# Closing an expert's first tile earlier, and GpSimd's weight sums in four pieces

## The chip, the cores and the metric

The kernel runs on one core of a Trainium2 chip. The metric is the device time of one execution in microseconds (us); the time of a kernel is the median of its runs.

## The reference

Sliding window attention (8 batches, 8 heads, 576 tokens, head size 64, window 64), whose output becomes 4608 rows of 512, followed by a mixture of experts with 8 experts of which each token takes the best one:

```python
mask = (rel >= 0) & (rel < 64)
attn = softmax(where(mask, q @ k.T / 8, -1e9)) @ v     # per batch and head
x = attn.transpose(0, 2, 1, 3).reshape(4608, 512)
logits = x @ w_gate                                    # 512 x 8
e = argmax(logits); gate = softmax(logits)[e]
y[t] = gate[t] * (relu(x[t] @ w1[e]) @ w2[e])          # w1 512 x 1024, w2 1024 x 512
```

All inputs and outputs are f32.

## The kernel before

**Attention loop.** Batches are taken two at a time ("pairs", `bg`, four of them), heads two at a time. A pair has 9 column tiles of 128 tokens. A unit is one pair and two heads, and each unit takes three steps, so the loop has N = 48 steps (`step(s)`), software-pipelined: step s issues the scores of step s+1 (`scored`, L572) into PSUM banks 0 and 1, `weighted` (probabilities by v, L618) of step s-1, the logits of step s-3 (L655), the transposes of the probabilities of step s (`flipped`, L603), the division of step s-1 (`divided`, L628 to L632), the transposes of q and k for step s+3 (`turned`, L531 and L539) and of the attention output of step s-2 (`x_turned`, L643). On VectorE (DVE) each step has the mask and maximum (`masked`, L585), one copy of transposed probabilities (L605) and the division; on ScalarE (ACT) the exponentials (L595) and the other copies. GpSimd (POOL) makes shifted copies of v (L511 to L517).

**What else a step does** stands in the dictionary `todo`: a list of operations for each step, run at the end of that step in the order in which they were appended. When the four logit products of a pair are done, `after` puts its routing there: the parts of the generator `choose(bg)` (expert, rank among the tokens of the expert, gate; each `next` runs up to a `yield`), then for each column tile `place` (L746: the matrix `lo` of one-hot lanes with the low digits of the token number, two DVE instructions), `weigh` (L757: the row times its gate) and `store` (L766, L773: the rows go to `x_dram`). The engines each run their own instructions in the order of issue, so an instruction that waits holds all behind it on its engine.

**Slots.** The tokens of an expert fill slots of tiles of 256. `slot_table` computes, once all four pairs are routed, which token sits in which slot: a one-hot matrix `hi` (L799), 72 small matmuls `lo` by `hi` (L807), and the table `perm_i` (L817). The first two tiles of expert 0 (`NE` = 2) don't wait for that table. `first_tiles` (called at step N-3 = 45) fills both from the first three pairs: `key`, `hi_e` (L859, L862), 54 matmuls (L869), `perm_e` (L872). Slots beyond the tokens at hand get a row number that is out of bounds, and `gather_first` (L280, L282) leaves zeros there; `count` of expert 0 is lifted to 512 after pair 2 (L730), so later tokens come behind.

**Expert products.** A tile of 256 tokens goes through one level of a Strassen-like scheme: `hidden` has 7 products (L322) and `output` 7 (L362), with `turn` (transposes of the gathered rows, L303, and two ACT copies, L304) and `sums_x` (four DVE sums of its quarters, L311) for the next tile in between. The sums of quarters of the weights are made by POOL: `sums_w1`, `sums_w2`, four instructions of 128 x 1024 each for each expert (L139). The same line 139 serves DVE for the four sums of the hidden quarters (128 x 512). `gather` (L270, L272) brings the rows of the tile after the next, `scatter` (L289, L292) writes results.

**Between the two phases** stands a tail whose order is written by hand: `tile0` is a generator of 15 items (7 products of tile 0's hidden layer, the turn of tile 1, 7 products of tile 0's output), and each `next(tile0)` puts one item between the last steps' attention work, the routing of the last pair and the slot table. Tile 1 follows, then the loop over experts with conditional blocks (L1028 to L1039). The weights w2 of expert 0 lie in the buffers of q and k (`qk_m`), their sums in those of the transposed q and k (`qkT_m`); the SP queue loads them in two halves put at steps N-6 and N-3.

Of the kernel before, what the change touches and what calls it, by code (L numbers as in the profile page):

```python
# [4 lines left out]

# [31 lines left out]
def kernel(  # L37
# [10 lines left out]
    nc = tc.nc  # L48
# [91 lines left out]

    def w1q(e):
        w = w1s[e % NW]
        return [w[:, a * HG : (a + 1) * HG, f * HD : (f + 1) * HD] for f in range(2) for a in range(2)]
# [5 lines left out]
    def sums_w1(e):  # L149
        form(left_sums(G, s1s[e % NW], *w1q(e)))  # L150

    def sums_w2(e):
        form(right_sums(G, s2s[e % NW], *w2q(e)))
# [59 lines left out]
    hi_e = rt.tile([P, NJE, NE * C], BF16, name="hi_e")  # L213
# [63 lines left out]
    def gather_first(tokens):  # L277

        for c in range(C):
            G.memset(xg[c], 0.0)  # L280

            G.indirect_dma_start(  # L282
                out=xg[c], out_offset=None, in_=x_dram[0 : NT - BG * S, :],
                in_offset=bass.IndirectOffsetOnAxis(ap=tokens[:, c : c + 1], axis=0),
                bounds_check=NT - BG * S - 1, oob_is_err=False,
            )
# [12 lines left out]
    def turn():  # L299
# [7 lines left out]
    def sums_x():  # L307
# [132 lines left out]
    with tc.manual_schedule(), ExitStack() as held, ExitStack() as brief:  # L440
# [236 lines left out]
        def choose(bg):  # L677
# [50 lines left out]
            if bg == last - 1:  # L728

                V.tensor_scalar_max(count[:, 0:1], count[:, 0:1], float(NE * TB))  # L730
# [48 lines left out]
        def slot_table(hi):  # L779
# [29 lines left out]
            for j in range(NJE):  # L809
                fill(j)  # L810
            for n in range(NST):
                for m in range(ST):
                    place(NJE + n * ST + m)
                yield
# [18 lines left out]
        def after(s, routing, bg):  # L833

            do = lambda n, op: todo.setdefault(s + n, []).append(op)
            part = lambda: next(routing, None)
            if bg < last - 1:
                for n in range(5):
                    do(n, part)

                for m in range(NTB):
                    do(5 + m * 2 // 3, partial(place, bg * NTB + m))
                    do(5 + m * 2 // 3, partial(weigh, bg, m, G))
                    if m % ST == ST - 1:
# [12 lines left out]
        def first_tiles():  # L857

            V.scalar_tensor_tensor(  # L859
                out=key[:], in0=rkhi[:, 0:NJE], scalar=1.0, in1=oh_all[:, 0, 0:NJE], op0=ALU.add, op1=ALU.mult  # L860
            )
            V.tensor_tensor(  # L862
                out=hi_e[:], in0=_inner(key[:], NE * C), in1=_ins(hi_id[:, C + 1 : C + 1 + NE * C], 1, NJE),
                op=ALU.is_equal,
            )
            slots = banks[next(tr_ring)](0, NE * C)
            for j in range(NJE):
                for i in range(2):
                    nc.tensor.matmul(  # L869
                        slots, lhsT=lo[:, i, j], rhs=hi_e[:, j], start=(i + j == 0), stop=(i + j == NJE)  # L870
                    )
            V.tensor_scalar(out=perm_e[:], in0=slots, scalar1=-1.0, scalar2=float(NT), op0=ALU.mult, op1=ALU.add)  # L872
            gather_first(perm_e[:, 0:C])
# [16 lines left out]
        for n, op in enumerate(left_sums(G, s1s[0], *w1q(0))):  # L890
# [86 lines left out]
        next(tile0)  # L977
        next(routing, None)
        weigh_some(2)
# [90 lines left out]
```

## Time and profile before

| | |
|---|---|
| median of 3 runs | 763.73 us (763.55 to 766.46) |
| profiled execution, time | 765.36 us |
| its span, first to last instruction | 763.5 us |
| mean granted TensorE clock | 0.989 |
| busy PE, DVE, POOL, ACT | 722.8, 397.0, 357.0, 268.3 us |
| POOL sums of the weights, 128 x 1024 | 2.35 to 2.54 us each (means of the groups) |

The profile is of one execution. Busy time is the union of the recorded instructions of an engine. Beside an instruction stands the idle time of its engine just before it, and in an arrow what ended that wait; "PEclk" is the share of full clock that TensorE was granted.

### The profile page before, as it was taken

The page shows a single profiled execution, that of the slowest core. Times are in us where ns is not written, and L with a number is a line of the kernel's source. Part 1 is how long each engine was busy: PE and PEld are TensorE (multiplying, and loading weights), DVE is VectorE, ACT ScalarE, POOL GpSimd, SP SyncE. Part 2 cuts the span into 40 slices and gives each one's busy share as a digit, 9 for nine tenths or more (in the row PEclk, how much of TensorE's full clock was granted, in tenths as well). Part 3 has the DMA queues.
Part 4 walks back from the last instruction along what each step waited for, and adds up shares of the span by engine and source line. Part 5 has one row for each costly group of instructions (what it writes and reads, how often), then busy time and mean ns, then how long its engine had stood idle before and what let it go on. Part 6 is the DMA issues. An engine that isn't in the chain of part 4 may idle for free. (4 is left out here: it accounts for less than half of the span.)

```text
span 763.5 us, 18251 instructions
## 1 busy us (share of the span) xinstructions
PE 722.8 (95%) x7018; PEld 651.8 (85%) x7018; DVE 397.0 (52%) x1355; ACT 268.3 (35%) x676; POOL 357.0 (47%) x366
## 2 busy tenths in 40 slices
PE   5999999998899989999999999999999999999995
PEld 3878888887688978988999899899998899988994
DVE  2666998988748554434533452352434452424432
ACT  4778888897634201211220121111220121202220
POOL 5214668485770544546531553663256465262111
PEclk9999999999899999999999999999999999999998
DMA  7998889794513711702501170441161171101101
GB/s 161 210 201 183 190 183 257 175 236 128 181 56 125 276 57 32 264 29 93 203 32 54 48 257 30 141 164 56 44 247 53 35 258 56 41 25 42 43 28 55
DMA packets 137616, 94.48 MB, mean 124 GB/s; under 512 B 117072, under 2 KB 117072, under 8 KB 137490
## 3 DMA queue, kind: packets, MB, share of 16 engines
q1 hardware_dynamic: 127858, 62.16, 29.6%
q0 software_dynamic: 9056, 28.58, 11.3%
q10 hardware_dynamic: 576, 2.10, 0.9%
q8 instruction: 74, 1.21, 0.6%
q14 instruction: 52, 0.43, 0.2%
HBM read 73.94 MB, written 20.45 MB: 124 GB/s over the span
## 5 line engine op out<-in xcount | busy, mean ns | idle before, releaser
L322 PE MATMUL bank<-qk_m,s 128*128 128x128 f32 x1216 | 145.6, 275 | 0.0
L322 PEld LDWEIGHTS bank<-qk_m,s 128*128 128x128 f32 x1216 | 140.5, 192 | 0.1
L322 PE MATMUL bank<-qk_m,w 128*128 128x128 f32 x912 | 112.5, 276 | 10.7 <-DVE v_m L358 7.1
L272 POOL DMA_INDIRECT qk_m<-x_dram,at_g x42 | 44.6, 1061 | 166.3 <-PE bank L303 159.0
L322 PEld LDWEIGHTS bank<-qk_m,w 128*128 128x128 f32 x912 | 106.8, 192 | 15.9 <-issue 15.7
L595 ACT ACTIVATE pr<-pr,mx 128x128 f32<-128x128 f32 x288 | 89.7, 391 | 34.2 <-DVE mx L585 31.8
L358 DVE TENSOR_TENSOR v_m<-bank,v_m 128x256 f32<-128x256 f32 x101 | 40.9, 422 | 110.3 <-PE bank L362 54.8
L585 DVE CUSTOM_DVE_ANT_0 pr<-bank,mask 128x128 f32<-128x128 f32 x288 | 64.4, 286 | 28.2 <-PE bank L572 25.8
L292 POOL DMA_INDIRECT out_dram<-v_m,at_s x42 | 42.4, 1009 | 60.7 <-DVE v_m L358 49.0
L329 ACT COPY qk_m<-bank 128x512 f32<-128x512 f32 x19 | 11.2, 587 | 164.2 <-PE bank L322 135.0
L139 POOL TENSOR_TENSOR s<-w 128x1024 f32<-128x1024 f32 x22 | 52.3, 2377 | 17.6 <-DMA qk_m<-x_dram,at_g 17.6
L362 PE MATMUL bank<-qkT_m,v_m 128*128 128x256 f32 x240 | 54.0, 380 | 1.7 <-DVE v_m L139 1.7
L362 PEld LDWEIGHTS bank<-qkT_m,v_m 128*128 128x128 f32 x240 | 45.4, 190 | 8.6 <-DVE v_m L139 2.5
L513 POOL COPY v_m<-v_m 64x520 f32<-64x520 f32 x32 | 19.8, 618 | 69.3 <-DMA v_m<-in_v_dram 55.1
L362 PE MATMUL bank<-qk_m 128*128 128x256 f32 x224 | 52.1, 380 | 0.0
L618 PEld LDWEIGHTS bank<-v_m,pT 128*64 128x64 f32 x1152 | 41.2, 140 | 11.7 <-DVE xs L632 5.5
L618 PE MATMUL bank<-v_m,pT 128*64 128x65 f32 x1152 | 48.0, 231 | 2.7 <-DVE xs L632 2.7
L362 PE MATMUL bank<-s,v_m 128*128 128x256 f32 x216 | 48.1, 379 | 0.0
L362 PEld LDWEIGHTS bank<-qk_m 128*128 128x128 f32 x224 | 41.5, 190 | 5.5 <-ACT v_m L374 0.4
L362 PEld LDWEIGHTS bank<-s,v_m 128*128 128x128 f32 x216 | 41.0, 190 | 5.6
L572 PE MATMUL bank<-qkT_m 64*64 64x128 f32 x1152 | 45.4, 289 | 0.1
L539 PE MATMUL bank<-ident,qk_m 128*128 128x128 f32 x256 | 35.9, 283 | 8.5 <-DMA qk_m<-in_q_dram 6.3
(167 smaller groups left out, 1223.8 us busy)
## 6 DMA issues: line engine op xcount, KB each, us to landing
w<-in_moe_w_dram SPq DMA_DIRECT2D x11, 2048.0 KB, 9.4
qk_m<-in_q_dram SPq DMA_DIRECT2D x72, 128.0 KB, 3.4
qk_m<-in_k_dram SPq DMA_DIRECT2D x72, 128.0 KB, 3.4
v_m<-in_v_dram SPq DMA_DIRECT2D x64, 128.0 KB, 3.8
qk_m<-in_moe_w_dram SPq DMA_DIRECT2D x3, 2048.0 KB, 15.3
x_dram<-xs POOLq DMA_DIRECT2D x6, 512.0 KB, 4.7
x_dram<-xs POOLq DMA_DIRECT2D x3, 768.0 KB, 5.0
w<-in_moe_w_dram ACTq DMA_DIRECT2D x4, 512.0 KB, 4.4
```

Of the source, the lines that this page charges most:

```text
L139: op()
L272: G.indirect_dma_start(out=xg[c], out_offset=None, in_=x_dram[:, :], in_offset=bass.IndirectOffsetOnAxis(ap=at_g[:, c : c + 1], axis=0),)
L292: put = G.indirect_dma_start(out=out[:, :], out_offset=bass.IndirectOffsetOnAxis(ap=at_s[:, c : c + 1], axis=0), in_=ys[c], in_offset=None ...
L322: nc.tensor.matmul(acc[:, f, :], lhsT=a[:, g, f * P : (f + 1) * P], rhs=b[:, g, :], start=(first and f == 0 and g == 0), stop=(g == HG - 1 ...
L358: plus = lambda out, a, b: V.tensor_tensor(out=out, in0=a, in1=b, op=ALU.add)
L362: nc.tensor.matmul(acc, lhsT=a[:, f, :], rhs=b[:, f, :], start=(start and f == 0), stop=(stop and f == HF - 1), skip_group_check=True,)
L513: nc.gpsimd.tensor_copy(out=vb[0:D, i].rearrange("p j h d -> p (j h d)"), in_=va[D:P, i].rearrange("p j h d -> p (j h d)"),)
L539: nc.tensor.transpose(out=tr.rearrange("d a b -> d (a b)").rearrange("d (p j) -> d j p", j=NV)[:, j, :], in_=t[:, c, j].rearrange("p h d - ...
L572: nc.tensor.matmul(out_, lhsT=qT[rows, t, a * WINDOW : (a + 1) * WINDOW], rhs=rhs, start=True, stop=True, skip_group_check=True,)
L585: V.tensor_tensor_reduce(out=prs[h][:, m, :], in0=scs[h][:, m, :], in1=mask[:, m0 + m, :], scale=-scale, scalar=-2 * MASKED, op0=ALU.add, ...
L595: nc.scalar.activation(out=y, in_=y, func=AF.Exp, scale=-1.0, bias=mx[:, h, m : m + 1])
L618: nc.tensor.matmul(px[a * D : (a + 1) * D, h, m, :], lhsT=pTs[h][:, m, a * D : (a + 1) * D], rhs=vt[:, h, :], start=True, stop=True, skip_ ...
```

## The change

1. `first_tiles` becomes `first_tile(n)`, a generator with one `yield` between the DVE part and the matmuls. Tile 0 takes tokens from the first two pairs (18 column tiles, 36 matmuls) and is made at steps N-10 and N-9; tile 1 takes them from the first three (54 matmuls) and is made in the tail. `gather_first` reads only the rows that belong to those pairs. `count` is lifted to 256 after pair 1 and to 512 after pair 2.
2. The routing of pair 2 is spread over other steps, and all its weighing is on POOL.
3. Tile 0's turn and `sums_x` run at step N-2, through PSUM banks 0 and 1; its first product and `sums_w2(0)` at step N-1. The tail has one `next(tile0)` less ahead of the loop of 8, `weigh_some(2)` is later, and the slot table's 54 early matmuls come two items later.
4. The two w2 loads of expert 0 are put one step earlier.
5. POOL's sums of w1 and w2 are issued in four instructions each, along the last dimension (w1: 128 x 2 x 128, w2: 128 x 4 x 64 elements).

```diff
+    def pieces(engine):
+
+        def tensor_tensor(op, **aps):
+            n = aps["out"].shape[-1] // 4
+            for i in range(4):
+                engine.tensor_tensor(op=op, **{name: ap[:, :, i * n : (i + 1) * n] for name, ap in aps.items()})
+        return SimpleNamespace(tensor_tensor=tensor_tensor)
...
-        form(left_sums(G, s1s[e % NW], *w1q(e)))
+        form(left_sums(pieces(G), s1s[e % NW], *w1q(e)))
...
-        form(right_sums(G, s2s[e % NW], *w2q(e)))
+        form(right_sums(pieces(G), s2s[e % NW], *w2q(e)))
...
-            if bg == last - 1:
-
-                V.tensor_scalar_max(count[:, 0:1], count[:, 0:1], float(NE * TB))
+            if last - NE <= bg < last:
+
+                V.tensor_scalar_max(count[:, 0:1], count[:, 0:1], float((bg - last + NE + 1) * TB))
...
-            for j in range(NJE):
-                fill(j)
             for n in range(NST):
                 for m in range(ST):
                     place(NJE + n * ST + m)
+                if n == 1:
+                    for j in range(NJE):
+                        fill(j)
                 yield
...
-            for n in (0, 0, 1, 2, 2):
+            for n in (0, 1, 1, 2, 3):
                 do(n, part)
             for m in range(NTB):
-                do(3 + m // 3, partial(place, bg * NTB + m))
-                do((2, 2, 3, 3, 4, 4, 4, 5, 5)[m], partial(weigh, bg, m, nc.scalar if m in (2, 6) else G))
+                do((4, 4, 5, 5, 6, 6, 7, 7, 7)[m], partial(place, bg * NTB + m))
+                do((2, 3, 3, 4, 4, 5, 5, 6, 6)[m], partial(weigh, bg, m, G))
                 if m % ST == ST - 1:
-                    do(3 + m // ST, partial(store, bg, m // ST, G))
-            do(6, first_tiles)
+                    do(4 + m // ST, partial(store, bg, m // ST, G))
-        def first_tiles():
+        def first_tile(n):
+            nj = (last - NE + n + 1) * NTB
             V.scalar_tensor_tensor(
...
+            yield
+            slots = banks[next(tr_ring)](0, C)
+            for j in range(nj):
                 for i in range(2):
                     nc.tensor.matmul(
...
+            to = perm_e[:, n * C : (n + 1) * C]
+            V.tensor_scalar(out=to, in0=slots, scalar1=-1.0, scalar2=float(NT), op0=ALU.mult, op1=ALU.add)
+            gather_first(to, nj * P)
+            yield
...
-        for n, s in enumerate((N - 6, N - 3)):
+        for n, s in enumerate((N - 7, N - 4)):
...
+        tile0 = chain(hidden(0), turn(), output(0))
+        first = first_tile(0)
+        todo.setdefault(N - 10, []).append(partial(next, first))
+        todo.setdefault(N - 9, []).append(partial(next, first))
+        free = [banks[i](0, NG, P) for i in (0, 1)]
+        todo.setdefault(N - 2, []).extend((lambda: form_all(turn(free)), partial(sums_x, free)))
+        todo.setdefault(N - 1, []).extend((partial(next, tile0), partial(sums_w2, 0)))
         for s in range(-3, N):
             step(s)
-        sums_w2(0)
         tr_ring = cycle((4, 5))
-        tile0 = chain(hidden(0), turn(), output(0))
         px = weighted(N - 1, pTs.pop(N - 1))
-        form_all(turn())
         logit(N - 3)
         divided(N - 1, px)
         x_turned(N - 2)
-        sums_x()
-        gather_first(perm_e[:, C : 2 * C])
+        second = first_tile(1)
+        next(second)
+        next(tile0)
         by_tok = [by_tokens(last, c) for c in range(NST)]
         next(by_tok[0])
-        next(tile0)
         logit(N - 2)
         x_turned(N - 1)
+        next(second)
...
         weigh_some(1)
-        next(tile0)
         next(routing, None)
-        weigh_some(2)
         next(tile0)
...
-        for _ in range(8):
+        for n in range(8):
             next(tile0)
             next(table, None)
+            if n == 1:
+                weigh_some(2)
```

More of the change, by code (lines that the diff above doesn't have):

```diff
@@ L4 @@
 from itertools import chain, cycle
+from types import SimpleNamespace
 import concourse.bass as bass
@@ L212 @@
     key = rt.tile([P, NJE], BF16, name="key")
-    hi_e = rt.tile([P, NJE, NE * C], BF16, name="hi_e")
+    hi_e = rt.tile([P, NJE, C], BF16, name="hi_e")
     at_b = rt.tile([P, NJ], BF16, name="at_b")
@@ L275, in gather, with gather_first @@
             )
-    def gather_first(tokens):
+    def gather_first(tokens, rows):
         for c in range(C):
@@ L282, in gather_first @@
             G.indirect_dma_start(
-                out=xg[c], out_offset=None, in_=x_dram[0 : NT - BG * S, :],
+                out=xg[c], out_offset=None, in_=x_dram[0:rows, :],
                 in_offset=bass.IndirectOffsetOnAxis(ap=tokens[:, c : c + 1], axis=0),
-                bounds_check=NT - BG * S - 1, oob_is_err=False,
+                bounds_check=rows - 1, oob_is_err=False,
             )
@@ L297, in scatter, with turn @@
             tc.add_to_no_dep_group("puts", put.ins)
-    def turn():
+    def turn(tps=tps):
         for c in range(C):
@@ L305, in turn, with sums_x @@
         yield
-    def sums_x():
+    def sums_x(tps=tps):
         b12, b22, b21 = tps[1][:, 0:HG], tps[1][:, HG:], tps[0][:, HG:]
@@ L846, in after @@
                 return
-            for n in (0, 0, 1, 2, 2):
+            for n in (0, 1, 1, 2, 3):
                 do(n, part)
             for m in range(NTB):
-                do(3 + m // 3, partial(place, bg * NTB + m))
-                do((2, 2, 3, 3, 4, 4, 4, 5, 5)[m], partial(weigh, bg, m, nc.scalar if m in (2, 6) else G))
+                do((4, 4, 5, 5, 6, 6, 7, 7, 7)[m], partial(place, bg * NTB + m))
+                do((2, 3, 3, 4, 4, 5, 5, 6, 6)[m], partial(weigh, bg, m, G))
                 if m % ST == ST - 1:
-                    do(3 + m // ST, partial(store, bg, m // ST, G))
-            do(6, first_tiles)
-        def first_tiles():
+                    do(4 + m // ST, partial(store, bg, m // ST, G))
+        def first_tile(n):
+            nj = (last - NE + n + 1) * NTB
             V.scalar_tensor_tensor(
-                out=key[:], in0=rkhi[:, 0:NJE], scalar=1.0, in1=oh_all[:, 0, 0:NJE], op0=ALU.add, op1=ALU.mult
+                out=key[:, 0:nj], in0=rkhi[:, 0:nj], scalar=1.0, in1=oh_all[:, 0, 0:nj], op0=ALU.add, op1=ALU.mult
             )
             V.tensor_tensor(
-                out=hi_e[:], in0=_inner(key[:], NE * C), in1=_ins(hi_id[:, C + 1 : C + 1 + NE * C], 1, NJE),
-                op=ALU.is_equal,
-            )
-            slots = banks[next(tr_ring)](0, NE * C)
-            for j in range(NJE):
+                out=hi_e[:, 0:nj], in0=_inner(key[:, 0:nj], C),
+                in1=_ins(hi_id[:, (n + 1) * C + 1 : (n + 2) * C + 1], 1, nj), op=ALU.is_equal,
+            )
+            yield
+            slots = banks[next(tr_ring)](0, C)
+            for j in range(nj):
                 for i in range(2):
                     nc.tensor.matmul(
-                        slots, lhsT=lo[:, i, j], rhs=hi_e[:, j], start=(i + j == 0), stop=(i + j == NJE)
+                        slots, lhsT=lo[:, i, j], rhs=hi_e[:, j], start=(i + j == 0), stop=(i + j == nj)
                     )
-            V.tensor_scalar(out=perm_e[:], in0=slots, scalar1=-1.0, scalar2=float(NT), op0=ALU.mult, op1=ALU.add)
-            gather_first(perm_e[:, 0:C])
+            to = perm_e[:, n * C : (n + 1) * C]
+            V.tensor_scalar(out=to, in0=slots, scalar1=-1.0, scalar2=float(NT), op0=ALU.mult, op1=ALU.add)
+            gather_first(to, nj * P)
+            yield
         N = NU * NST
@@ L889 @@
             )
-        for n, op in enumerate(left_sums(G, s1s[0], *w1q(0))):
+        for n, op in enumerate(left_sums(pieces(G), s1s[0], *w1q(0))):
             todo.setdefault(3 * NST + n, []).append(op)
```

## The prediction

> **What bounds the kernel now.** The page comes first: TensorE (PE) is busy 95% of the span, the next engine 52%. So only a moment in which PE stands still, or runs below full clock, is worth time. I then read the list of waits of PE, summed the busy time by stretch, and opened the timeline where the sum was short. PE busy over 175.68 to 278.41 us (the last seven steps of the attention loop, the tail with tile 0, tile 1) is 91.90 of 102.73 us; from there to 755.60 it is 466.36 of 477.19. A tenth of the first stretch is lost and 2% of the second, which holds 17 of the 19 full tiles. The change touches the first stretch.
>
> From the busy time by stretch; columns are the stretch, its length, busy us (count) of PE, weight load, DVE, ACT, POOL, then PE's granted clock, DMA share, GB/s. These are steps 42, 45, 46 and 47 (a step starts on PE with the scores of the next one, L572; step 47, which has none, with `weighted`, L618):
> ```profile
> 184.44:190.14 5.70, 4.29 (x73) 3.45 (x72) 5.25 (x30) 2.75 (x10) 0.39 (x1) 1.00 0.00 0
> ...
> 197.62:206.19 8.57, 5.27 (x119) 4.33 (x118) 6.83 (x34) 5.00 (x16) 7.73 (x9) 0.89 0.68 241
> 206.19:212.25 6.06, 5.43 (x67) 4.37 (x64) 2.89 (x17) 2.72 (x8) 3.12 (x4) 0.59 0.31 101
> 212.25:215.58 3.33, 2.45 (x39) 1.95 (x40) 1.38 (x4) 0.86 (x2) 3.25 (x2) 1.00 0.25 79
> ```
> Step 42 leaves PE idle 1.41 us while DVE is full; step 45 leaves it idle 3.30 us; the next runs at clock 0.59. The timeline of step 45 shows why (start, length, engine, line; in brackets the idle time before it and what ended it):
> ```profile
> 201.49 0.49 PE L643 MATMUL bank<-ident,xs 128*128 128x128 f32 x3
> 204.68 1.58 PE L869 MATMUL bank<-hi_e,lo 128*128 128x4 bf16 x54 [2.70 <-DVE hi_e L862]
> 206.19 1.56 PE L572 MATMUL bank<-qkT_m 64*64 64x128 f32 x24
> ```
> The 54 slot matmuls of `first_tiles` stand in PE's order and wait for `hi_e`, which DVE makes last in that step, after six lo's and the softmax work. PE stood 2.70 us, and in slices of half a microsecond its clock is 0.50 from about 204.4 to 211.05. Under it L572 took 1.56 for 0.89, L618 1.62 for 0.97, L655 0.65 for 0.42, L603 1.49 for 0.88: 2.2 us lost beside the gap.
>
> Tile 1's output, PE then DVE then POOL:
> ```profile
> 269.41 1.99 PE L362 MATMUL bank<-qkT_m,v_m 128*128 128x256 f32 x8 [0.94 <-DVE v_m L139]
> 272.17 3.72 PE L362 MATMUL bank<-qkT_m,v_m 128*128 128x256 f32 x16 [0.76 <-DVE v_m L139]
> ...
> 263.89 2.71 DVE L139 TENSOR_TENSOR v_m<-qk_m 128x512 f32<-128x512 f32 x1 [0.75 <-ACT qk_m L350]
> 266.64 2.72 DVE L139 TENSOR_TENSOR v_m<-v_m,qk_m 128x512 f32<-128x512 f32 x1
> 269.28 2.83 DVE L139 TENSOR_TENSOR v_m<-qk_m 128x512 f32<-128x512 f32 x1
> ...
> 263.71 2.35 POOL L139 TENSOR_TENSOR s<-s,w 128x1024 f32<-128x1024 f32 x1
> 266.02 2.79 POOL L139 TENSOR_TENSOR s<-w 128x1024 f32<-128x1024 f32 x1
> ```
> DVE's sum takes 0.69 us alone (median 692 ns) and 2.7 beside a sum on POOL: the two take turns, whole instruction by whole instruction, and PE waits 1.70 us for the result.
>
> [...]
>
> **The change, part by part.**
> 1. *Tile 0 closed at steps 38 and 39.* At step 39 come 18 x 2 = 36 matmuls at 28 ns (1.51 us from 204.68 to 206.19 over 54): +1.0 us of PE. `key` and `hi_e` (0.18 + 0.27 us at most) are made one step earlier, so PE does not wait; the lo's of pair 1 were done at 168.9, before step 39 (171.53). Out of step 45 go the 54 matmuls (1.5), the gap (2.70) and the slow clock. On POOL, two memsets and two indirect DMAs (0.54, 1.12, 0.55, 1.02) go behind the v copies, which end at 179.89; the store they read lands at about 179.3 (175.30 + 0.56 + 3.4). So the weighing begins near 183.2 and not 181.72; nine weighings at 1.56 and stores of 4.1 us end near 201.5, where before POOL stood 8.1 us for ACT's weighing and ended at 205.14. Nothing on PE reads x_dram before the tile 1 gather.
> 2. *Routing of pair 2 spread out.* The fourth part moves to step 41 (DVE busy 2.48 of 3.42), so step 42 loses most of its 1.41 us and step 41 grows by some 0.8. Two lo's leave step 45 for step 46. I take steps 40 to 45 as 5.3 + 4.2 + 4.2 + 4.1 + 3.4 + 3.6 = 24.8 us, against 30.5 (175.68 to 206.19). With the +1.0: **-4.7 us**. The one-step-earlier w2 loads are free: the first was issued at 179.53, when its buffer's last transposes had run, and that does not move.
> 3. *Tile 0's turn at step 46, its first product at step 47*, with POOL's w2 sums. PE at full clock: step 46 3.05 + turn 0.95; step 47 0.9 + 0.35 + 0.6 + 0.4 + product 1.8: 8.05 us. DVE in step 46: 2.9, sums_x 1.6, six lo's at 0.22 alone (1.35 us) or, if each waits for a piece, 0.65 (3.9): with 1.5 for step 47, 7.4 to 9.9 us. I take 8.8 against the 9.39 before (206.19 to 215.58): **-0.6**. The turn writes the score banks; DVE has read them 1.5 us after the scores, the turn comes 2.9 us after.
> 4. *The tail* (215.58 to the first product of tile 1 at 249.66, 34.1 us). Ahead of the last `choose` PE loses turn and product (1.02 + 1.9), gains 54 slot matmuls (1.5), and one later product moves ahead of it (1.8): it starts 10.2 us in, not 9.85. From there DVE was busy 21.40 of 24.62; it loses one 0.69 sum, and the wait of 1.29 us for `hi` at L807 goes, since the fills come later. PE alone would need 21.1 (24.6 less 1.8, 1.29 and a wait of 0.42 for y1), DVE with most of its waits 23.5; I take 22.5. Sum 32.7: **-1.4**. The last weighing and its store come two products later, some 4 us; they landed 10 us ahead of the gather at 251.14, so this costs nothing and frees ACT for the relus. Tile 1's gather: w2 sums from about 203.5 (last scores read) to 214.7, slots ready near 216.5, memsets and indirect DMAs 3.3 us, landing 3.4 (both as at 221.18 to 223.82): 223.2. Its turn comes near 226, so it is hidden by 3 us.
> 5. *Pieces.* A piece costs between 0.59 us (a quarter) and 0.77 (0.19 us fixed, from the slope of the copies L513 and L517, plus 0.04 between two); I take 0.70. Four sums take 11.2 us, not 9.4. In tile 1 the DVE sums wait a piece each, 1.35 us: they end at 265.2, 266.6, 267.9 and are needed at 268.4 and 270.2; **-1.5** of the 1.70. In the other tiles the growth of 1.8 us is hidden: no PE wait is ended by POOL in the list of waits but for the masks at the start, and POOL idles 159.0 us for L303. Expert 1's w2 sums start at 298.83, their last result is used about 320.6: 21.8 us for 11.2.
>
> Sum: -4.7 - 0.6 - 1.4 - 1.5 = -8.2 us. The profiled execution took 765.36 with a span of 763.5, 1.63 above the median of 763.73; its span would be 755.3, the median **755.5**.
>
> **Rivals.**
> *The wait moves to DVE.* For it: DVE is busy 20.20 of the 21.94 us from 175.68 to 197.62. Then the steps before 45 save nothing (-2.7), steps 46 and 47 cost DVE's 9.9 and 1.0 of starting late (+1.5), the tail needs DVE's 23.5 (-0.4), tile 1 gives -1.0: -2.6, 761.1. Against it: the work that DVE gains is 2 us and some of it falls where PE had waited for it.
> *Nothing is left of the waits.* PE idle 10.83 in the stretch, slow clock 2.2, less 1.0 of new matmuls and the 0.8 at 278.41 that is a block's start: -11.2, 752.5.
> *Slower: POOL becomes the bound through the pieces.* Place: the w2 sums of seven experts. It decides from 21.8 / 16 = 1.36 us a piece, where the product at 320.6 begins to wait. At 1.6 us it costs 0.24 x 16 x 7 = 27 us: 782.5. For it: the trace has no small two-input sum. Against: a fixed cost of 1 us would show in the copies, which take 0.30.
> *The change adds tiles.* If pairs 0 and 1 held under 256 tokens of expert 0, slots would stay empty. Counting the reference's own routing gives 265 + 156, and 538 after pair 2: 19 full tiles and 2 half ones either way, as L329 x19 says. No chance.
>
> **Numbers.** Forecast case 0.62 (own range 753 to 759.5), nothing left 0.03, wait on DVE 0.23 (a third of it past the bound), POOL 0.12 with whatever I don't see. Faster by over 0.5%, which is 3.8 us and about what a measurement here can tell: 0.62 + 0.03 + 0.07 = 0.72; same 0.16; slower 0.12. The range runs from PE's floor, 752.5, past the DVE case to 764.
>
> **What would show it.** Right: no PE idle over 1 us between the scores of steps 45 and 47 and a clock of 1.00 there; the last scores near 201.5, `weighted` of the last step near 210.3, tile 1's first product near 243.0; pieces of 0.65 to 0.75 us; DVE L139 never over 1.6 us. Wrong: PE waiting for pT or lo at steps 46 and 47; the tile 1 turn (near 226) waiting for its gather, which I expect landed at 223.2; pieces over 1.3 us; a clock below 1.00 anywhere near.

## The result: 7% slower, and the profile after

The changed kernel takes **818.05 us** (median of four runs, 813.96 to 820.81), beside 764.35 for the kernel before: ratio 1.069, 95% interval 1.064 to 1.074. Its profiled execution took 817.94 us with a span of 816.2, 52.7 us more than the 763.5 of before. Line numbers moved: L303 of before is L312 now, L322 is L331, L358 is L367, L362 is L371, L572 is L581, L585 is L594, L618 is L627, L746 is L755; POOL's pieces are L147, DVE's sums L140.

Cut at the points that the prediction used, in us by the profiles:

| stretch | before | predicted | after |
|---|---|---|---|
| to the scores of the last step (L581) | 206.19 | 201.5 | 202.81 |
| steps 46 and 47, to the last `weighted` | 9.39 | 8.8 | 19.50 |
| tail, to tile 1's first product | 34.08 | 32.7 | 32.63 |
| tile 1 | 28.75 | 27.25 | 26.52 |
| the rest | 485.09 | as before | 534.74 |

Three stretches came near their forecasts. One lost 10.1 us, and the rest, which was to stay as it was, lost 49.7. From the busy time by stretch (length, then busy us and count of PE, weight load, DVE, ACT, POOL, then PE's clock):
```profile
202.81:222.31 19.50, 10.24 (x128) 8.53 (x127) 17.98 (x38) 6.18 (x17) 11.38 (x17) 0.82 0.10 35
...
254.94:281.46 26.52, 25.72 (x177) 23.95 (x178) 12.19 (x24) 4.78 (x9) 18.67 (x25) 1.00 0.56 199
281.46:816.20 534.74, 481.56 (x3200) 445.21 (x3200) 243.09 (x344) 85.09 (x161) 232.16 (x326) 0.95 0.25 85
```
In the last row PE is idle 53.18 us (534.74 less 481.56), and was 18.73 before: 34.45 more. It is also busy 15.20 longer with the same 3200 matmuls, at a clock of 0.95. The list of PE's waits (total, times, longest) names the idle part at once:
```profile
PE bank L371 <- DVE v_m L367: 34.8, 6, 5.8
PE bank L331 <- DVE v_m L367: 9.5, 12, 1.4
PE bank L312 <- DVE mx L594: 8.5, 1, 8.5
```
Six waits of 5.8 us for DVE, one for each of the w1 sums of experts 2 to 7. The arrow names the instruction that came last, L367, which is an ordinary addition; what held it up stands ahead of it on DVE (in the case below L367 starts at 337.88, behind a sum that ends at 336.52). The costliest groups of the page show it, the fourth sum of the hidden quarters:
```profile
L140 DVE TENSOR_TENSOR v_m<-qk_m,v_m 128x512 f32<-128x512 f32 x19 | 80.4, 4230 | 0.0
```
A mean of 4230 ns for an instruction whose median is 684 is six long ones among thirteen short ones. The timeline of one (start, length):
```profile
338.36 3.78 PE L371 MATMUL bank<-w,v_m 128*128 128x256 f32 x8 [5.81 <-DVE v_m L367]
...
324.68 11.84 DVE L140 TENSOR_TENSOR v_m<-qk_m,v_m 128x512 f32<-128x512 f32 x1
...
323.85 1.15 POOL L281 DMA_INDIRECT qk_m<-x_dram,at_g  x1 [0.30 <-issue]
325.02 2.77 POOL L147 TENSOR_TENSOR s<-w 128x256 f32<-128x256 f32 x4
...
333.21 2.75 POOL L147 TENSOR_TENSOR s<-w,s 128x256 f32<-128x256 f32 x4
```
DVE's sum stands from just ahead of POOL's first piece to just after its last: not one turn in sixteen pieces. PE's 5.81 us of idling are followed by a clock of 0.50, and the eight matmuls take 3.78 us, twice the 1.89 that eight such take at full clock (at 358.70 in this profile):
```profile
338.36:347.60 9.24, 8.39 (x29) 7.16 (x30) 2.03 (x5) 0.58 (x1) 2.22 (x3) 0.50 0.16 59
```
Step 46 shows the same with another DVE instruction, one `lo` of 0.30 us, which comes a microsecond into the run of the w2 pieces:
```profile
214.86 1.97 PE L312 MATMUL bank<-ident,qk_m 128*128 128x128 f32 x8 [8.51 <-DVE mx L594]
...
203.70 9.34 DVE L755 TENSOR_SCALAR lo<-lane,low,tok_a 128x128 bf16<-128x128 bf16 x1
...
202.14 0.56 POOL L782 DMA_DIRECT2D x_dram<-xs  x1
202.72 2.79 POOL L147 TENSOR_TENSOR qkT_m<-qk_m 128x256 f32<-128x256 f32 x4
```
But in tile 1 the very same code shares as forecast. There POOL first stood 5.20 us waiting for a DMA to land and then made a small copy, DVE's sums come in the middle of the run and take 1.0 to 1.2 us, and the four pieces beside them grow from 2.77 to 4.58:
```profile
272.36 1.21 DVE L140 TENSOR_TENSOR v_m<-qk_m,v_m 128x512 f32<-128x512 f32 x1
...
266.70 0.18 POOL L279 COPY at_g<-perm_i 128x2 int32<-128x2 int32 x1 [5.20 <-DMA qk_m<-x_dram,at_g]
266.85 2.77 POOL L147 TENSOR_TENSOR s<-w 128x256 f32<-128x256 f32 x4
269.58 4.58 POOL L147 TENSOR_TENSOR s<-s,w 128x256 f32<-128x256 f32 x4
```
So the question for the experiments: when does POOL give DVE a turn?

### The profile page after: what moved, and what is told of

Read it like the earlier page. It is cut to its first block, busy times and chain, and to the rows that moved or that the text cites. A ratio compares the mean times of both kernels' runs of the same rounds, so it can differ in the third digit from the quotient of the medians.

```text
span 816.2 us, 18522 instructions
## 1 busy us (share of the span) xinstructions
PE 738.5 (90%) x7054; PEld 662.2 (81%) x7054; DVE 454.3 (56%) x1359; ACT 266.9 (33%) x674; POOL 385.8 (47%) x560
## 3 DMA queue, kind: packets, MB, share of 16 engines
q0 software_dynamic: 9056, 28.58, 10.6%
## 5 line engine op out<-in xcount | busy, mean ns | idle before, releaser
L331 PE MATMUL bank<-qk_m,s 128*128 128x128 f32 x1216 | 145.8, 276 | 0.0
L331 PEld LDWEIGHTS bank<-qk_m,s 128*128 128x128 f32 x1216 | 141.2, 193 | 0.0
L331 PE MATMUL bank<-qk_m,w 128*128 128x128 f32 x912 | 114.2, 279 | 10.3 <-DVE v_m L367 9.5
L331 PEld LDWEIGHTS bank<-qk_m,w 128*128 128x128 f32 x912 | 108.4, 194 | 16.7 <-issue 16.3
L367 DVE TENSOR_TENSOR v_m<-bank,v_m 128x256 f32<-128x256 f32 x101 | 40.9, 422 | 100.7 <-PE bank L371 49.7
L140 DVE TENSOR_TENSOR v_m<-qk_m,v_m 128x512 f32<-128x512 f32 x19 | 80.4, 4230 | 0.0
L594 DVE CUSTOM_DVE_ANT_0 pr<-bank,mask 128x128 f32<-128x128 f32 x288 | 64.3, 286 | 26.3 <-PE bank L581 24.9
L147 POOL TENSOR_TENSOR s<-w 128x256 f32<-128x256 f32 x96 | 66.5, 724 | 18.5 <-DMA qk_m<-x_dram,at_g 18.4
L371 PE MATMUL bank<-qkT_m,v_m 128*128 128x256 f32 x240 | 53.7, 379 | 0.0
L371 PE MATMUL bank<-qk_m 128*128 128x256 f32 x224 | 52.1, 380 | 0.0
L371 PEld LDWEIGHTS bank<-qkT_m,v_m 128*128 128x128 f32 x240 | 45.5, 190 | 6.1
L627 PEld LDWEIGHTS bank<-v_m,pT 128*64 128x64 f32 x1152 | 41.3, 140 | 11.1 <-DVE xs L641 5.0
L627 PE MATMUL bank<-v_m,pT 128*64 128x65 f32 x1152 | 48.1, 231 | 1.8 <-DVE xs L641 1.3
L371 PE MATMUL bank<-s,v_m 128*128 128x256 f32 x216 | 48.1, 379 | 0.0
L371 PEld LDWEIGHTS bank<-qk_m 128*128 128x128 f32 x224 | 41.5, 190 | 5.5 <-ACT v_m L383 0.4
L371 PEld LDWEIGHTS bank<-s,v_m 128*128 128x128 f32 x216 | 41.0, 190 | 5.6
L341 DVE TENSOR_TENSOR qk_m<-bank,qk_m 128x512 f32<-128x512 f32 x19 | 13.1, 692 | 58.2 <-PE bank L331 53.5
```

The costliest lines, as they stand in the source:

```text
L140: op()
L147: engine.tensor_tensor(op=op, **{name: ap[:, :, i * n : (i + 1) * n] for name, ap in aps.items()})
L331: nc.tensor.matmul(acc[:, f, :], lhsT=a[:, g, f * P : (f + 1) * P], rhs=b[:, g, :], start=(first and f == 0 and g == 0), stop=(g == HG - 1 ...
L341: V.tensor_tensor(out=u2, in0=y, in1=p1, op=ALU.add)
L367: plus = lambda out, a, b: V.tensor_tensor(out=out, in0=a, in1=b, op=ALU.add)
L371: nc.tensor.matmul(acc, lhsT=a[:, f, :], rhs=b[:, f, :], start=(start and f == 0), stop=(stop and f == HF - 1), skip_group_check=True,)
```

## The experiments

### Which part costs

`e1_whole` is the changed kernel with whole sums; `e2_pieces` is the kernel before with nothing but the pieces.
```diff
 # e1_whole
-            n = aps["out"].shape[-1] // 4
-            for i in range(4):
+            n = aps["out"].shape[-1]
+            for i in range(1):
```


> The whole change, but each of POOL's weight sums in one instruction of 1024 elements as before. Theory A (a DVE instruction with two SBUF inputs[...] that meets a run of short POOL sums gets no turn until the run is over): the six DVE sums of 11.8 us fall back to about 3.3 us, PE's six waits of 5.8 us and the slow clock behind them go (-49.7 us from 281.46 on), and the lo's at step 46 wait for at most one whole sum each. I expect 757 to 763 us, below the kernel before. Theory B (closing tile 0 earlier overloads steps 46 and 47 and the tail, and that is what costs): still above 764. Theory C (POOL as a whole became too slow through the pieces): about as theory A in the second phase, so this run alone doesn't part A from C.

> The kernel before with nothing but the sums in four pieces each. Theory A: the six waits in the second phase are all there, about 8.3 us each, and tile 1 gains its 2.2: 764.4 + 49.7 - 2.2 = 812 us, with six DVE sums of about 11.8 us. Theory B: within 5 us of before. Theory C: well above before, with PE or DVE waiting for POOL's sums or scatter instead of DVE's fourth sum being long.

Measured: `e1_whole` 765.57 us, ratio 1.0022 (1.0010 to 1.0034); `e2_pieces` 806.47, ratio 1.0553 (1.0508 to 1.0599). The pieces alone make the loss. The rest of the change alone gains nothing, though: `e1_whole` lies above its forecast of 757 to 763, because steps 46 and 47 take 15.26 us in it (9.39 before), where `lo` instructions beside whole sums take up to 2.38 us each. That is more than the loop and the tail give back. `e2_pieces` was expected at 812. In it five of the six sums take 11.8 us; in the expert that escapes, the sum had begun at 527.85, 0.93 us ahead of the run at 528.78, and was over (0.69 us) when the run began. In `e1_whole` the sums take 3.27 us as before:
```profile
L140 DVE TENSOR_TENSOR v_m<-qk_m,v_m 128x512 f32<-128x512 f32 x19 | 28.5, 1499 | 0.0
```
The profile of before has 1500 there. It was a first sign: 3.27 us is about one whole sum on POOL and then DVE's own 0.69, and DVE got in just where POOL's second sum reads the first (in the profile of before POOL's first ends at 324.23, the second starts at 324.31, and DVE's sum, begun at 321.53, ends at 324.79).

### Length or order

`e3_by_piece` keeps the sixteen pieces and puts them in another order: all four sums of piece 0, then of piece 1, so that the second instruction of every four reads the one just ahead of it. `e7_w2_pieces` is the kernel before with pieces for w2 alone, with sixteen instructions for four in seven experts but not where the six long sums were; beside the w2 pieces DVE's additions read a PSUM bank, and in the changed kernel they kept their time there (0.42 us at 302.09 and 303.75, beside pieces from 301.84 on; the 101 of that line, L367, lie between 0.41 and 0.43). `e6_before_by_piece` is the kernel before with both in the new order.
```diff
 # e3_by_piece; e6_before_by_piece puts the same into the kernel before
+    def form_by_piece(sums, s, quarters):
+        n = s.shape[-1] // 4
+        for i in range(4):
+            cut = slice(i * n, (i + 1) * n)
+            form(sums(G, s[:, :, :, cut], *[q[:, :, cut] for q in quarters]))
...
-        form(left_sums(pieces(G), s1s[e % NW], *w1q(e)))
+        form_by_piece(left_sums, s1s[e % NW], w1q(e))
...
```


> The whole change with the same 16 pieces of a set of sums, in another order: for each piece the four sums one after the other, so that the second and the fourth sum of a piece read what POOL wrote one and two instructions before. Theory A1 (the run gives no turn because each piece starts before the one ahead has ended, and only a dependence between neighbours opens a gap): DVE's fourth sum waits for two pieces at most, under 2.5 us, PE's 5.8 us waits are gone, 755 to 760 us. Theory A2 (short instructions starve DVE whatever their order): the fourth sum stays near 11.8 us and the time near 818. Theory C (POOL's length): POOL's sums cost as much or more, no change, near 818.

> The kernel before with nothing but the pieces in the order by piece. Theory A: no DVE sum over 1.7 us, tile 1 shorter by the 2.2 us seen in both kernels with pieces, the rest as before: 762 us (761 to 763). Theory C (pieces lengthen POOL and cost by that): 764 or more.

> The kernel before with only the w2 sums in four pieces, in the order of the change; w1 in whole sums. In the second phase no DVE instruction with two SBUF inputs stands beside a w2 set, while POOL's sets get longer by 1.6 us as in the change. Theory A: no change, 764 us within 1.5. Theory C (POOL's length): half of the loss of 42 us, near 785.

Measured: `e3_by_piece` 764.10 us, ratio 0.9999 (0.9986 to 1.0012); `e7_w2_pieces` 764.27, ratio 1.000 (0.9984 to 1.0017). The order is worth 54 us, and the longer w2 sums of `e7_w2_pieces` cost nothing. `e3_by_piece` missed its 755 to 760 all the same: its steps 46 and 47 take 13.16 us, since most `lo` instructions beside the run wait for a piece (0.77 us and not 0.31). In `e3_by_piece` the six sums take 1.65 us, the rest of the first piece and their own time:
```profile
L140 DVE TENSOR_TENSOR v_m<-qk_m,v_m 128x512 f32<-128x512 f32 x19 | 19.3, 1015 | 0.0
```
In one of them POOL's first piece ends at 320.08, the second, which reads it, starts at 320.15, and DVE's sum ends at 320.64: DVE gets its turn at the gap that the dependence opens. `e6_before_by_piece` took 765.92, ratio 1.0025 (1.0013 to 1.0036), where 762 was expected. Tile 1 has its gain there (26.5 us), but in its profile one body lasts 30.5 us instead of 26.4, with 2.2 us in which PE waits for nothing that the profile names, while two 2 MB loads of weights begin. Whether that one body is the whole of the miss stays open.

### A wait for DVE, and no meeting at step 46

`e4_after_dve` is the changed kernel in which POOL copies one element of DVE's fourth sum ahead of the w1 pieces of experts 2 to 7, and so waits for it. `e5_after_lo` is `e3_by_piece` in which POOL copies one element of the last early `lo` ahead of the w2 pieces of expert 0.
```diff
 # e4_after_dve
+    seen = consts.tile([P, 1], F32, name="seen")
...
+                if e:
+                    G.tensor_copy(out=seen[:], in_=hs[:, 3, HF - 1, P - 1 : P])
                 sums_w1(e + 1)
 # e5_after_lo
+    seen = consts.tile([P, 1], F32, name="seen")
...
-        todo.setdefault(N - 1, []).extend((partial(next, tile0), partial(sums_w2, 0)))
+        todo.setdefault(N - 1, []).extend((partial(next, tile0), lambda: G.tensor_copy(out=seen[:], in_=lo[:, 1, NJE - 1, P - 1 : P]), partial(sums_w2, 0)))
```


> The whole change with its pieces, but for experts 2 to 7 POOL first copies one element of DVE's fourth hidden sum (128 x 1) and so begins the w1 sums only when DVE has ended that sum; POOL's work is the same or more and ends later. Theory A (starved by the meeting): the six long DVE sums and PE waits go, while the loss at step 46 (8.5 us of waiting and its slow clock) stays: 818 - 49.7 = 768 us, between 766 and 771. Theory C (POOL too slow): no better than 818.

> The kernel with the pieces in the order by piece (e3), where POOL moreover copies one element of the last early lo (128 x 1) before the w2 sums of expert 0 and so begins them only when DVE has made all lo's. In e3 ten lo's took 0.77 us beside those sums and not 0.22, and steps 46 and 47 took 13.2 us against 8.8 predicted. Theory A (the meeting[...] is what is left of the loss): steps 46 and 47 fall to about 9 us, the last attention product (weighted of step 47) starts near 211, the whole is 4 us below e3: 760 us. Theory B (DVE is full there whatever POOL does, or the later sums push tile 1's gather onto PE's path): within 1 us of e3, 764, with a wait of PE elsewhere.

Measured: `e4_after_dve` 768.02 us, ratio 1.0056 (1.0039 to 1.0074), with no long sum and with the wait at step 46 left (10.2 us): some 50 us of the loss are the six sums. (POOL's run begins there only after the sum has ended, so this parts the two and shows no turn.) `e5_after_lo` 758.93, ratio 0.9922 (0.9902 to 0.9942): steps 46 and 47 fall from 13.16 us in `e3_by_piece` to 10.00, because the `lo` instructions take 0.31 again and not 0.77.

### What starves DVE

`m1_meeting` is a kernel of its own that only lets DVE instructions meet runs of POOL sums, without a DMA on POOL between them.

> The meeting by itself; attention and experts are left out, the output is zeros. 14 cases, each twice: POOL sums 4096 columns in instructions of 1024, 512, 256 or 128 columns, and one DVE instruction of 0.69 us (two SBUF inputs, 128 x 512) starts some 0.3 us ahead of the run (b), or once the k-th POOL instruction has ended (m). n4 and n2: every fourth or second POOL instruction reads the one before it. psum, copy, lo: the DVE instruction has one PSUM input, is a plain copy of f32, or has the form of the lo's. Theory A1 (back-to-back POOL instructions give no turn, whatever their size; a dependence between neighbours does): b1024, b512, b256, b128 all end only with the run, about 10 us, b256n4 after four pieces (2.8 us), b256n2 after two (1.4); psum256 0.69. Theory A2 (only short instructions starve DVE): b1024 about 3 us, b256 and b128 about 11. An instruction that comes in mid-run (m) gets no turn either under A1; in tile 1 of the changed kernel DVE's sums did, so I give this half and half.

Measured: no sum is starved. One that comes in the middle is served at the next boundary of pieces (0.93 us with pieces of 256, 1.73 with 512, 2.81 with 1024). The sums that were to stand ahead of the run took 0.68 us but did not meet it: the run begins when they are over, at 205.94 after an end at 205.93 in one of them. "Pieces that follow each other without a dependence starve DVE", which was the theory up to here, is false as it stands. What the starved runs have besides is a DMA that POOL issued just ahead. The theory became: behind such a DMA a run whose pieces don't read each other gives DVE no turn, unless POOL first waits for a result of its own. Its rival in `e8_settle`: sixteen pieces without a dependence give none, whatever stands ahead. `m2_lead` varies the lead, and `e8_settle` puts two one-element instructions between DMA and pieces in the changed kernel:
```diff
+    once, twice = (consts.tile([P, 1], I32, name=n) for n in ("once", "twice"))
+
+    def settle():
+        G.memset(once[:], 0)
+        G.tensor_copy(out=twice[:], in_=once[:])
...
-        todo.setdefault(N - 1, []).extend((partial(next, tile0), partial(sums_w2, 0)))
+        todo.setdefault(N - 1, []).extend((partial(next, tile0), settle, partial(sums_w2, 0)))
...
+                if e:
+                    settle()
                 sums_w1(e + 1)
```


> A kernel of its own: it computes nothing of the reference and writes zeros. Fourteen trials, each twice: on GpSimd one lead instruction (an indirect gather of 128 rows of 2 KB, a plain load of 128 rows, or a 128x512 copy), then a run of 16 pieces of 256 or 4 sums of 1024 elements of two tiles; on VectorE one 128x512 sum (0.68 us alone) that becomes ready about when the run begins, or once piece 1 or 9 is there. In trials with n2 or n4 every second or fourth piece reads the piece before. Theory[...]: after gather or load, VectorE's sum lasts to the end of the run, 10 to 11 us where it comes at the start, some 9 from piece 1, some 4 from piece 9, 9 to 10 us for four sums of 1024; n4 2 to 3 us; n2 1 to 1.7 us; sums of 1024 with n2 3 us; with two small instructions, of which the second reads the first, between gather and run 0.7 to 1.4 us; after a copy 0.7 to 1.4 us. First rival (a sum that waits when the run begins is starved whatever leads; one that comes in the middle gets its turn): after the copy 10 us too, and from pieces 1 and 9 below 1.4 us whatever leads. Second rival (it takes what the real kernel has besides: TensorE's and ScalarE's work, or its addresses): every sum below 1.8 us, 3 for sums of 1024.

> The changed kernel, with two one-element instructions on GpSimd, of which the second reads the first, ahead of the sums of w1 of experts 2 to 7 (after the gather is issued) and ahead of the sums of w2 of expert 0 (after the stores of x). Nothing waits for VectorE, and the sixteen pieces follow each other as before. Theory[...]: the fourth hidden sums take 0.7 to 1.5 us in all six experts, no lo near step 46 takes over 1.6 us, no wait at the output products or at the turn is over 2 us; lo's cost some 4 us at steps 46 and 47 as with the order piece by piece: 761 to 766 us. Rival[...]: fourth sums 11.8 us, 817 us. Second rival (only what the sum on VectorE meets at the very start matters, so the two instructions only move the start by 0.3 us and give VectorE its turn first): fourth sums 0.7 us, but the lo at step 46, which comes in the middle of a run, still takes 9 us: 768 us.

Measured: `e8_settle` **762.95 us**, ratio 0.998 (0.9967 to 0.9993). Two instructions of 0.12 and 0.19 us take the loss of 54 us away. Step 46, where the `lo` comes in the middle of the run:
```profile
204.62 0.81 DVE L761 TENSOR_SCALAR lo<-lane,low,tok_a 128x128 bf16<-128x128 bf16 x1
...
203.07 0.56 POOL L788 DMA_DIRECT2D x_dram<-xs  x1
203.63 0.12 POOL L272 MEMSET once<- 128x1 int32 x1
203.81 0.19 POOL L273 COPY twice<-once 128x1 int32<-128x1 int32 x1
203.97 2.79 POOL L147 TENSOR_TENSOR qkT_m<-qk_m 128x256 f32<-128x256 f32 x4
```
0.81 us in place of 9.34. Not all is as expected, though. A later `lo` beside the last four pieces of the same run got no turn at three boundaries, and `weighted` then waited 2.59 us for DVE; no `lo` was to take over 1.6 us:
```profile
212.79 2.71 DVE L761 TENSOR_SCALAR lo<-lane,low,tok_a 128x128 bf16<-128x128 bf16 x1
...
212.21 2.79 POOL L147 TENSOR_TENSOR qkT_m<-qkT_m,qk_m 128x256 f32<-128x256 f32 x4
```
And the six sums take 0.68 us without meeting the run: in one expert the sum ends at 320.65 and the run begins at 320.67.

In `m2_lead`, after a plain load a sum that comes after piece 1 takes 9.76 us, after a copy 0.93:
```profile
172.65 9.76 DVE L60 TENSOR_TENSOR dma256at1x<-s,db 128x256 f32<-128x256 f32 x1 [2.33 <-POOL s L56]
211.15 0.93 DVE L60 TENSOR_TENSOR copy256at1x<-s,db 128x256 f32<-128x256 f32 x1 [2.19 <-POOL s L56]
```
After a gather a sum that waits at the run's start takes 11.82, four sums of 1024 10.11, and 1.63 or 2.97 where every second or fourth piece reads its neighbour. From pieces 1 and 9 after the gather it takes 0.94 and 3.67, which is a miss. The first rival is out all the same: the lead decides.

`m3_between` asks whether a wait is needed between DMA and run, or any instruction will do. The core of it:
```python
def run(size, near):
    for i in range(W // size):
        at = slice(i * size, (i + 1) * size)
        prior = slice((i - 1) * size, i * size)
        in0 = s[:, prior] if near and i % near == near - 1 else wa[:, at]
        G.tensor_tensor(out=s[:, at], in0=in0, in1=wb[:, at], op=ALU.add)
...
if pre.startswith("dma"):
    G.dma_start(out=xg[n % 2][:], in_=rows[0:P, :])
if pre.endswith("settle"):
    G.memset(tick2[:], 1.0)
    G.tensor_copy(out=tick3[:], in_=tick2[:])
if pre.endswith("apart"):
    G.memset(tick2[:], 1.0)
    G.tensor_copy(out=tick3[:], in_=db[:, 0:1])
```

> Again a kernel of its own that writes zeros: 16 pieces of 256 (once 8 of 512) on GpSimd, and VectorE's 128x256 sum (0.93 us with a turn at the next boundary) becomes ready when piece 1, 2, 5 or 9 is there. Leads: a plain load that GpSimd issues, an indirect gather, none. Between lead and run: nothing; two one-element instructions of which the second reads the first (settle); two that don't read each other (apart); one 128x512 copy (long). In one trial piece 7 reads piece 6. Theory[...]: after the load 9 to 10 us from piece 1, some 7 from 5, some 4 from 9, 9 us or more from piece 0 of 512; 3.5 to 4.5 us where piece 7 reads 6; settle 0.9 us after load and gather; apart and long still 7 us or more; no lead 0.9 us. Rival ([...]any instruction after it lets go): apart and long 0.9 us as settle. After the gather the run before this one gave 0.94 us from piece 1 and 3.67 from piece 9, which neither expects: from 2 and 5 the theory gives 9 and 7 us[...].

The timeline, DVE's sum after piece 1, then what POOL had between the plain load and the run (settle, then apart):
```profile
91.33 0.93 DVE L60 TENSOR_TENSOR dmasettle256n0at1x<-s,db 128x256 f32<-128x256 f32 x1 [2.60 <-POOL s L56]
104.19 9.77 DVE L60 TENSOR_TENSOR dmaapart256n0at1x<-s,db 128x256 f32<-128x256 f32 x1 [2.46 <-POOL s L56]
219.47 9.75 DVE L60 TENSOR_TENSOR dma256n0at1y<-s,db 128x256 f32<-128x256 f32 x1 [2.35 <-POOL s L56]
...
89.58 0.12 POOL L74 MEMSET tick<- 128x1 f32 x1
89.76 0.18 POOL L75 COPY tick<-tick 128x1 f32<-128x1 f32 x1
...
102.57 0.12 POOL L77 MEMSET tick<- 128x1 f32 x1
102.61 0.20 POOL L78 COPY tick<-db 128x1 f32<-128x1 f32 x1
```
With settle the copy starts 0.06 us after the end of the memset that it reads; apart, it starts 0.08 us before. That is the difference in time between the two, and it is 0.93 against 9.77 us, both times that each trial ran; one 128x512 copy in between helps no more (9.77), though at 0.62 us it delays the run by more than settle does, so the delay is not the cure. Where piece 7 reads piece 6 the sum takes 3.64 us: served at that dependence. In the first of the two plain trials (0.93 us, where 9.75 is shown for the second) the run itself first waited 32.76 us for a load of its data; that this wait settled it is likely, but was not tried alone. After the gather, sums from pieces 1, 2 and 5 took 0.94 us, which the theory does not give.

So for the six sums of the real kernel, which follow gathers, one question was left: does settling help there, or only the 0.4 us by which it delays the run? `m4_start` lets the sum come at seven times around the run's start.

> A kernel of its own that writes zeros: an indirect gather that GpSimd issues, then nothing or the two small instructions of which the second reads the first (settle), then 16 pieces of 256; VectorE's 128x512 sum becomes ready at seven times from some 0.9 us ahead of the run to 0.7 us into it (short sums of 64 to 1088 elements go ahead of it). Theory[...]: without settle the VectorE instruction that is under way when the run begins takes 11 to 12 us; with settle none takes over 1.3 us, at any of the times. Rival (in the kernel with the two small instructions the sums on VectorE were only saved by the later start of the run, 0.4 us): with settle too the instruction that is under way when the run begins takes 11 to 12 us, at other widths than without.

Without settle, the DVE instruction at the run's start took about 11 to 12 us in six of the seven times, both rounds; in the seventh the sum was over before. With settle none was long; at five of the seven times the sum is over when the run begins, so the widths 896 and 1088 carry the test. The timeline without settle at 896, then with settle at 896 and 1088, where DVE is in the middle of an instruction when the run begins:
```profile
296.79 12.27 DVE L96 TENSOR_TENSOR dy<-da,db 128x512 f32<-128x512 f32 x2
394.04 0.68 DVE L60 TENSOR_TENSOR indsettlew896y<-da,db 128x512 f32<-128x512 f32 x1
408.87 1.22 DVE L60 TENSOR_TENSOR indsettlew1088y<-da,db 128x512 f32<-128x512 f32 x1
...
297.73 10.91 POOL L56 TENSOR_TENSOR s<-wa,wb 128x256 f32<-128x256 f32 x16
394.14 11.37 POOL L56 TENSOR_TENSOR s<-wa,wb 128x256 f32<-128x256 f32 x16
408.14 11.37 POOL L56 TENSOR_TENSOR s<-wa,wb 128x256 f32<-128x256 f32 x16
```
The run gives way: it lasts 11.37 us and not 10.91. The rival is out.

### The fastest version

`e9_best` is `e5_after_lo` with `settle()` ahead of the w1 pieces of experts 2 to 7.

> The kernel that was fastest so far (pieces in the order piece by piece, the sums of w2 of expert 0 behind the last early lo: 758.9 us), with the same two small instructions ahead of the sums of w1 of experts 2 to 7. Theory: the fourth hidden sum falls from 1.65 to some 0.7 to 1.2 us; as the hidden products cover 1.65 us already, the time stays within 1 us of 758.9. Rival (the 1 us of each sum is on the path of each body): 6 us less, 753.

Measured: 759.96 us, ratio 0.9938 (0.9919 to 0.9957); no fourth sum takes over 1.21 us. As expected the time stays at that of `e5_after_lo`: the 1.65 us were covered already. Both versions beat the kernel before, by 0.6 to 0.8%, and the changed one.

## Why the prediction was wrong, point by point

**Held.** Tile 1: -1.5 forecast, -2.2 measured; with whole sums (`e1_whole`) it is 28.58, so the pieces do bring that gain, by the turns that were forecast. Pieces: 0.70 us each and 11.2 for sixteen forecast, 10.9 to 11.0 measured. The tail: 32.7 forecast, 32.6 in the changed kernel and in its variants. Part of that match is luck: PE was to wait some 1.4 us for DVE there (22.5 taken for 21.1 of its own), and it was idle only 0.58 us (32.05 busy of 32.63).

**Right way, half the size: the loop.** Forecast -4.7 us, measured -3.4 here. But the unchanged loop itself varies: its last scores begin at 203.73 to 206.31 in the four profiles that have it (mean 205.3), and at 200.51 to 205.60 in the seven with the changed loop (mean 202.9). About -2.4 is left, no more than the spread.

**Failed: step 5, "In the other tiles the growth of 1.8 us is hidden", with "the DVE sums wait a piece each".** I asked only whether POOL's longer work ended a wait of PE, and `e7_w2_pieces` shows that this part was right. I did not ask what DVE meets there. From tile 1's timeline I took that the two engines take turns, whole instruction by whole instruction, and carried it to eighteen other tiles. In six of them DVE's fourth sum was already 3.27 us before the change, and the list of DVE's groups of before shows it, a mean far above the 0.69 us that the prediction took:
```profile
L139 DVE TENSOR_TENSOR v_m<-qk_m,v_m 128x512 f32<-128x512 f32 x19 | 28.5, 1500 | 0.0
```
What the runs showed in its place: behind the gather that POOL issues, the run of pieces, none of which reads the one just ahead, gave DVE's sum no turn at all, 11.84 us and not one piece of waiting. The prediction's own sign, "DVE L139 never over 1.6 us", failed in all six. The price is 34.45 us of PE waits and 15.20 of slower matmuls.

**Failed: step 3, "if each waits for a piece, 0.65".** One `lo` took 9.34 us, by the same cause: 19.50 us for 8.8. Some of the miss is independent of it. With whole sums the two steps take 15.26, with the order by piece 13.16, with settle 13.89, and with no piece beside the `lo`s still 10.0; the forecast was 1.2 us short even there, which turns the -0.6 of that step into +0.6.

**The slower rival named the right engine and the wrong mechanism**: pieces that cost over 1.36 us. They cost 0.68 one after the other. A rival of the other kind was there to be had: the one unknown of the change was how sixteen short instructions of POOL and one of DVE take turns, and I bounded it at one piece from the only place where it was harmless.

**What explains it.** Shown by the runs: three things stood together wherever DVE was held for most of a run, namely a DMA issued by POOL ahead, pieces back to back, and no piece that reads the one just ahead. Without the DMA (a copy as lead, or none) the sum took 0.93 us against 9.76. With it, each of two remedies gave DVE its turn: a wait of POOL for its own result ahead of the run (settle, 0.93 us against 9.77), or pieces that read their neighbour (every second, fourth or eighth: 1.63, 2.97 and 3.64). Shortness is not the cause: four independent sums of 1024 held DVE for 10.11 us behind a gather. What the change took away is the neighbour that reads: with whole sums the second reads the first, with pieces each reads the one four places back.

Not shown: what is different inside POOL behind a DMA. The overlap of neighbouring pieces doesn't tell the runs apart: it is 0.04 us in the starved run at 325.02 (0.724 us each, one every 0.683) and 0.04 in a run of `m1_meeting` without any DMA (three of 0.72 in 2.08). Nor does the length: in `m4_start` sixteen pieces take 10.91 us, whether they hold DVE (widths 384 to 1088, without settle) or begin, settled, when its sum is over (64 to 768). And turns by whole instruction, read from 0.69 against 2.71 us before the change, are too little for these runs, in which DVE stood for sixteen.

**Open.** Behind a gather, every sum that was held for the run had begun just ahead of it; one that arrives in the middle is mostly served (0.94 us from pieces 1, 2 and 5; 3.67 from 9), while behind a plain load it was not: but for the first trial of `m3_between`, it lasted to the run's end (9.75 us from piece 1, 7.06 from 5, 4.33 from 9). And in `e8_settle` a `lo` went without a turn for 2.71 us although the run had been settled. No run here explains either.

## What to carry to other kernels

Cutting GpSimd's work into short pieces gave VectorE a turn at the next boundary (0.93 us) where no DMA from GpSimd's queue led the run, and none in sixteen pieces to six sums behind a gather (11.84 us). There, put a small instruction that waits for GpSimd's own previous result ahead of the run (818.05 us became 762.95), or order the pieces so that neighbours depend on each other (764.10). Of the two, the small instruction still left one wait of 2.71 us. Where the order of work allows it, keeping the two engines' work apart helped beyond either: `e5_after_lo`, which adds that to the second, takes 758.93 us, where the two alone take 762.95 and 764.10. When a duration is carried from one place of a trace to another, look at the instruction's minimum, median and mean over all places first; here a mean of twice the median (1500 against some 690 ns) was the mark of six sums that met something else.

## What was not expected of the hardware

- A 128x512 sum on VectorE took 0.68 us alone, 1.2 beside pieces with turns, 3.27 beside whole sums and 11.84 beside pieces without turns.
- Two one-element GpSimd instructions, the second reading the first, were worth 55 us (818.05 against 762.95).
- After 5.81 us of idling TensorE ran at clock 0.50 for 9.2 us.
